# Second layer of the last two token tiles by seven block products each

## The chip, the cores and the metric

The kernel runs on one core of a Trainium2 chip. TensorE (PE) multiplies matrices, VectorE (DVE), ScalarE (ACT) and GpSimd (POOL) work elementwise, SyncE (SP) issues most transfers. Each engine takes its instructions in the order of the program and waits for the others by semaphores. The metric is the device time of one execution in microseconds; the kernel before takes 279.55 us (median of 3 runs, 279.43 to 279.59).

## The reference

Linear attention over 8 batches of 8 heads, 576 tokens and 64 columns a head, then two matrix layers with a leaky ReLU between them:

```python
q_s = softmax(q, axis=-1); k_s = softmax(k, axis=2)
kv = np.einsum('bhsd,bhse->bhde', k_s, v)
x = np.einsum('bhsd,bhde->bhse', q_s, kv)   # as 4608 tokens x 512
h = x @ w_in                                # 512 -> 2048
g = np.maximum(0.01 * h, h)
return g @ w_out                            # 2048 -> 512, float32
```

## The kernel before

The 4608 tokens are nine tiles of 512 (0 to 8). Attention fills `xT` (bf16, 128 partitions x 4 blocks of columns x 4608 tokens) some tiles ahead of the two layers. The first layer of a tile is 16 blocks of 128 of the 2048 hidden columns, four matmuls each, and a leaky activation by ACT into `g` tiles; the second layer is four groups of 128 tokens (`tsub`), 16 matmuls of 512 columns each, summed in one PSUM bank. All of it is bf16. The program is scheduled by hand: each engine's order is the order of the code.

The last two tiles, 7 (`TA`) and 8 (`TB`), go another way. The first layer of both together is a product of 2 x 2 blocks (tokens of tile 7 and 8; halves of the 512 input columns; hidden columns j and 8 + j), and Winograd's form needs seven block products for it, not eight, at the price of sums of blocks. Weight sums t1 to t4 come from GpSimd (`in_weight_sums`, L789; `last_weights`, L827, casts the block b22), token sums s1 to s4 from DVE (`token_sums`), stored as f32 (`F32R`); five of the seven products have such sums as operands, two are plain bf16. `pair_layer1(i)`, for i from 0 to 7, is one *block row*: seven products of two matmuls of 512 columns (`product`, L967), seven adds on DVE (L989), and four leaky activations. `pair_first(i + 1)` makes the first product of the next row and copies it by ACT to `e1` (L976). The last leaky of a row is held back into the next one (`held_leaky`). The hidden results go to `g7` (tile 7) and `g8` (tile 8), most of them into parts of `xT` that are no longer needed (`spent`).

Between the products PE gets *filling* matmuls, taken one by one from a generator (`fill_steps`): 48 of tile 6's second layer (`tsub` 1 to 3), then 16 of tile 7's (`pair_step`, L1027), eight a block row. Behind the last row come tile 7's other 48 matmuls (L1027) and its stores. Meanwhile DVE and ACT make the sums r1 to r4 and c22 of tile 8's hidden block for its second layer (L1070 to L1075). That layer is again a 2 x 2 product (halves of 256 tokens; halves of 2048 hidden columns; halves of 512 output columns) by seven products `product2` (L1091) of 16 matmuls of 256 columns: two in bf16 and five in f32, with weight sums v1 to v4 and o22 made earlier (`out_weight_sums`). DVE adds them up (L1101) and the results are stored (`put`, L1112).

PSUM: `psB_pool` has six banks, taken in turn, for every product; `psO_pool` has two, for the second layer's groups. A product waits until the bank of the sixth one before has been read. The raw input buffers (`raw_pool`, six) are taken over by the weight sums through `strip`; the pools of the attention part (`front`) are closed before `token_sums`, and the pools of the pair stage (`pairs`) before the last stage.

Of the kernel before, what the change touches and what calls it, by code (L numbers as in the profile page):

```python
# [20 lines left out]
L = 64  # L21
R = 9
# [4 lines left out]
def kernel(  # L27
# [37 lines left out]
    mx_pool = front.enter_context(tc.tile_pool(name="mx", bufs=1))  # L65
    small_pool = front.enter_context(tc.tile_pool(name="small", bufs=3))
    qT_pool = front.enter_context(tc.tile_pool(name="qT", bufs=2))

    psB_pool = ctx.enter_context(tc.tile_pool(name="psB", bufs=6, space=bass.MemoryType.PSUM))
    psO_pool = ctx.enter_context(tc.tile_pool(name="psO", bufs=2, space=bass.MemoryType.PSUM))  # L70
# [43 lines left out]


    XH, X8, XE = (slice(0, 7), slice(9, 16)), slice(7, 9), slice(16, 20)
    qe1 = const_pool.tile([P, XE.stop, P], BF16, name="qe1")
    vb2 = [const_pool.tile([P, R, 2, 2, D + 2], BF16, name=f"vb{i}") for i in range(2)]
# [689 lines left out]

    def in_weight_sums(i):
        w = lambda cs, fh: w_in_sb[:, cs, (fh * NH + i) * P : (fh * NH + i + 1) * P]  # L810
        if i == 0:
            late["t"] = strip("t")
# [17 lines left out]

    def token_sums():
        front.close()
        late["one"] = pool = pairs.enter_context(tc.tile_pool(name="late", bufs=1, reuse_waits="tile"))
        late["pool"] = pairs.enter_context(tc.tile_pool(name="late2", bufs=2, reuse_waits="tile"))
        for n in ("s1", "s2", "s3", "s4", "a22"):
# [124 lines left out]

    g7 = {}
    g8 = spent

    def product(w, a):
        ps = psB_pool.tile([P, TT], FP32, name="pp", tag=BANK_TAG)
# [12 lines left out]
    def pair_layer1(i, between):  # L978
# [3 lines left out]
        if i < 2:  # L982
            pair = g_pool.tile([P, 2, TT], BF16, name="gj")
            g7[i], g7[NH + i] = pair[:, 0], pair[:, 1]
        else:
            g7[i], g7[NH + i] = (spent(NF + 2 * (i - 2) + n) for n in range(2))

        def add(o, ps, e):
            nc.vector.tensor_tensor(out=o, in0=ps, in1=e, op=ALU.add)  # L989

        def do(w, a):
            ps = product(w, a)
            next(between)
            return ps

        add(u2, do(of(("t2", i)), of("s2")), e1)
        for fn in held_leaky:
            fn()
        add(e1, do(lambda c: w_in_sb[:, 2 + c, i * P : (i + 1) * P], lambda c: xT[:, 2 + c, XA]), e1)
        leaky(g7[i], e1)  # L1000
        add(u3, do(of(("t3", i)), of("s3")), u2)
        p5 = do(of(("t1", i)), of("s1"))
        add(u4, p5, u2)
        if i + 1 < NH:
            pair_first(i + 1)
            next(between)
# [4 lines left out]
        add(u3, do(of(("t4", i)), of("a22")), u3)  # L1011
        leaky(g8(i), u3)
        add(u4, do(of(("b22", i)), of("s4")), u4)
        held_leaky[:] = [lambda: leaky(g7[NH + i], u4)]
        if i + 2 < NH:
            in_weight_sums(i + 2)

    pouts, started = {}, [0] * NTS
    turn = [j for i in range(NH) for j in (i, NH + i)]

    def pair_step(tsub):
        j = turn[started[tsub]]
        started[tsub] += 1
        if tsub not in pouts:
            pool, tag = (psO_pool, "pout") if tsub < 2 else (psB_pool, BANK_TAG)
            pouts[tsub] = pool.tile([P, O], FP32, name="pout", tag=tag)
        nc.tensor.matmul(  # L1027
            pouts[tsub],
            lhsT=g7[j][:, tsub * P : (tsub + 1) * P],
            rhs=w_out_sb[:, j],  # L1030
            start=(started[tsub] == 1),
            stop=(started[tsub] == NF),
        )

    def fill_steps():
        for tsub in range(1, NTS):
            yield from layer2_at(TA - 1, g_sb, tsub)
        for tsubs in ((2, 3), (0, 1)):
            for _ in range(4):
                for tsub in tsubs:  # L1040
                    pair_step(tsub)
                    yield

    def between_products():
        fill = fill_steps()
        for n in range(NH):
            for k in range(7):
                for _ in range(1 + k // 6):
                    next(fill)
                yield  # L1050

    between = between_products()
    pair_first(0)
    next(between)
    for i in range(NH):
        pair_layer1(i, between)
    held_leaky[0]()
    next(between, None)
    pairs.close()
    pool = ctx.enter_context(tc.tile_pool(name="late3", bufs=1, reuse_waits="tile"))  # L1060
    quarter = lambda h, b, fh: xT[:, :, (2 * fh + b) * TT + h * M2 : (2 * fh + b) * TT + (h + 1) * M2]
    for n in ("r1", "r2", "r3", "r4", "c22"):
        late[n] = pool.tile([P, NH, M2], F32R, name=n)
    for first in (True, False):
        for b in range(2):
            o = lambda n: late[n][:, 4 * b : 4 * b + 4]
            part = lambda n: o(n).bitcast(FP32)
            a11, a12, a21, a22 = (quarter(h, b, fh) for h in range(2) for fh in range(2))
            if first:
                nc.scalar.copy(out=o("c22"), in_=a22)  # L1070
                nc.vector.tensor_tensor(out=o("r1"), in0=a21, in1=a22, op=ALU.add)
                nc.vector.tensor_tensor(out=o("r2"), in0=part("r1"), in1=a11, op=ALU.subtract)
            else:
                nc.vector.tensor_tensor(out=o("r3"), in0=a11, in1=a21, op=ALU.subtract)
                nc.vector.tensor_tensor(out=o("r4"), in0=a12, in1=part("r2"), op=ALU.subtract)  # L1075

    while started[0] < NF:
        for tsub in range(NTS):
            pair_step(tsub)
    for tsub in range(NTS):  # L1080
        store(TA * TT + tsub * P, pouts[tsub], nc.scalar.copy)

    def product2(a, w, each=False):
        if each:
# [15 lines left out]
    def add(o, ps, e):  # L1100
        nc.vector.tensor_tensor(out=o, in0=ps, in1=e, op=ALU.add)  # L1101

    rows = lambda n: (lambda m: late[n][:, m])
    plain_g = lambda fh: (lambda m: g8(fh * NH + m)[:, 0:M2])
    plain_w = lambda fh: (lambda m: w_out_sb[:, fh * NH + m, E1])
    out1, out2 = ([osb_pool.tile([P, O], FP32, name="out_sb") for _ in range(2)] for _ in range(2))
    e1, u2, u3, u4 = (g_pool.tile([P, 2, H2], FP32, name="gu", tag="gj") for _ in range(4))

    def put(o, half, i, cols):
        for n, issue in enumerate((nc.sync, nc.scalar)):  # L1110
            b, c = divmod(TB * TT + half * M2 + i * P + n * L, S)
            issue.dma_start(out=out_r[b, c // L, :, cols], in_=o[n * L : (n + 1) * L, cols])  # L1112

    nc.scalar.copy(out=e1, in_=product2(plain_g(0), plain_w(0)))
    ps = product2(plain_g(1), plain_w(1))
    for i in range(2):
        add(out1[i][:, E1], ps[:, i], e1[:, i])
        put(out1[i], 0, i, E1)
    add(u2, product2(rows("r2"), rows("v2")), e1)
    add(u3, product2(rows("r3"), rows("v3")), u2)  # L1120
    ps = product2(rows("r1"), rows("v1"))
    for i in range(2):
        add(out2[i][:, E2], ps[:, i], u3[:, i])
    add(u4, ps, u2)
    ps = product2(rows("c22"), rows("v4"))
    for i in range(2):
        add(out2[i][:, E1], ps[:, i], u3[:, i])
        put(out2[i], 1, i, slice(0, O))
    ps = product2(rows("r4"), rows("o22"), True)
    for i in range(2):  # L1130
        add(out1[i][:, E2], ps[i], u4[:, i])
        put(out1[i], 0, i, E2)
    assert not hooks, list(hooks)


# [28 lines left out]
```

## Time and profile before

| | before |
|---|---|
| median of 3 runs | 279.55 us |
| profiled execution | 279.63 us, of which the span from the first to the last instruction is 277.8 us |
| granted TensorE clock | 0.998 |
| TensorE weight loads (PEld) | 141.4 us, 51% of the span |
| HBM | 46 MB, 166 GB/s over the span |
| 210 to 249.8 us | block rows of tiles 7 and 8 with fillers |
| 249.8 to 260.2 us | tile 7's other 48 matmuls |
| 260.2 to 273.7 us | tile 8's seven products |
| 273.7 to 277.8 us | the last add and the last stores |

The profile is of one execution. Busy time is counted for each engine; a busy PE is not PE at its peak, as its matmuls are pipelined and their ends are modelled. In the timeline a matmul's time includes its way through the array, so successive starts tell its cost. The chain of waits follows the work that ended last back to its releaser. In rows of stretches the columns are PE, PEld, DVE, ACT and POOL (busy us and instructions), the clock, the DMA share and GB/s.

### The profile page before, as it was taken

How to read it: one execution, taken by the hardware profiler on the slowest of the kernel's cores; microseconds unless marked ns; L12 is line 12 of the kernel's file. 1: busy time of each engine (PE TensorE's matmuls, PEld its weight loads, DVE VectorE, ACT ScalarE, POOL GpSimd, SP SyncE). 2: the span in 40 equal slices, each digit the busy share in tenths (PEclk: the TensorE clock that was granted, in tenths of full speed). 3: DMA queues.
4: the chain of work that ended last, by engine and by line, in shares of the span. 5: the costliest groups of instructions: out<-in, count | busy, mean ns of one | idle time of the engine just before them, and what ended most of it. 6: DMA issues, size and time to landing. Idle time of an engine off the chain costs nothing.

```text
span 277.8 us, 5089 instructions
## 1 busy us (share of the span) xinstructions
PE 270.2 (97%) x1945; PEld 141.4 (51%) x1970; DVE 223.0 (80%) x310; ACT 166.2 (60%) x291; POOL 76.4 (28%) x97
## 2 busy tenths in 40 slices
PE   8899999999999999999999999999999999999994
PEld 3478644444444554445444444444445555554693
DVE  2986996999999959966885498967959999999542
ACT  4977573783488286755587448665674667655300
POOL 2957360159003002100500096003000856400000
PEclk9999999999999999999999999999999999999999
DMA  7999999987994499089409930330601011100243
GB/s 246 335 204 318 249 253 271 402 295 214 299 406 158 59 336 351 7 233 396 122 0 253 403 92 2 85 77 1 162 0 40 0 38 38 36 6 0 68 123 113
DMA packets 40167, 46.46 MB, mean 167 GB/s; under 512 B 18768, under 2 KB 23632, under 8 KB 40144
## 3 DMA queue, kind: packets, MB, share of 16 engines
q1 hardware_dynamic: 36160, 41.43, 47.5%
q0 software_dynamic: 3504, 4.20, 8.8%
q10 hardware_dynamic: 480, 0.52, 0.6%
q8 instruction: 15, 0.25, 0.3%
q14 instruction: 8, 0.07, 0.1%
HBM read 36.70 MB, written 9.44 MB: 166 GB/s over the span
## 4 chain that ended last, share of the span: by engine, by line
PE 93%; DVE 3%; DMA 2%; issue 1%; ACT 0%; SPq 0%; ACTq 0%
PE pout L583 35%; PE ph L562 35%; PE pp L967 9%; PE pout L1027 5%; PE pq L1091 5%; DMA k_raw<-in_k_dram 2%; PE po L478 2%; DVE t L159 1%; PE pokv L340 1%; PE pkv L340 1%; PE pkv L418 0%; DVE k_raw L409 0%; ACT ke L205 0%; DVE kmax L159 0%; ACT e L976 0%
## 5 line engine op out<-in xcount | busy, mean ns | idle before, releaser
L583 PE MATMUL pout<-w_out_sb,gj 128*128 128x512 bf16 x432 | 104.9, 380 | 1.0 <-issue 0.3
L562 PE MATMUL ph<-xT,w_in_sb 128*128 128x512 bf16 (+1 forms) x505 | 98.5, 352 | 0.4
L571 ACT ACTIVATE gj<-ph 128x512 bf16<-128x512 f32 x112 | 63.5, 602 | 19.1 <-PE ph L562 18.2
L562 PEld LDWEIGHTS <-w_in_sb 128*128 128x128 bf16 x512 | 49.7, 98 | 47.2 <-DMA w_in_sb<-in_moe_w_in_dram 0.3
L583 PEld LDWEIGHTS <-gj 128*128 128x128 bf16 x448 | 42.5, 98 | 54.8 <-issue 8.1
L217 POOL CAST vb<-v_raw 128x1152 bf16<-128x1152 f32 x13 | 21.8, 1707 | 81.9 <-DMA v_raw<-in_v_dram 81.9
L577 ACT COPY out_sb<-pout 128x512 f32<-128x512 f32 x28 | 16.0, 585 | 39.0 <-PE pout L583 20.4
L320 DVE TENSOR_REDUCE qsum<-qe 128x36 f32<-128x2304 bf16 (+5 forms) x13 | 20.0, 1542 | 6.2 <-ACT qe L311 6.1
L205 ACT ACTIVATE ke<-k_raw 128x2304 bf16<-128x2304 f32 (+2 forms) x13 | 18.0, 1383 | 9.4 <-DVE k_raw L197 9.0
L989 DVE TENSOR_TENSOR u<-pp,u 128x512 f32<-128x512 f32 x32 | 20.9, 685 | 1.4 <-PE pp L967 0.2
L327 DVE TENSOR_TENSOR qe<-qe,qrec 128x2304 bf16<-128x2304 bf16 (+5 forms) x13 | 21.5, 1657 | 0.4
L244 DVE TENSOR_REDUCE qmax<-q_raw 128x36 f32<-128x2304 f32 (+5 forms) x13 | 20.0, 1540 | 0.3 <-DMA q_raw<-in_q_dram 0.3
L311 ACT ACTIVATE qe<-q_raw 128x2304 bf16<-128x2304 f32 (+5 forms) x13 | 17.2, 1322 | 4.3 <-POOL q_raw L303 3.3
L967 PE MATMUL pp<-s,t 128*128 128x512 f32 x48 | 18.5, 486 | 0.0
L197 DVE TENSOR_TENSOR k_raw<-k_raw,kall 128x1152 f32<-128x1152 f32 (+2 forms) x10 | 18.1, 1821 | 0.3
L303 POOL TENSOR_TENSOR q_raw<-q_raw,qmax 128x512 f32<-128x512 f32 (+3 forms) x7 | 11.8, 1681 | 20.8 <-DVE qmax L244 20.3
L159 DVE TENSOR_TENSOR t<-t 128x256 f32<-128x256 f32 (+2 forms) x22 | 13.5, 615 | 0.7
L499 ACT CAST xT<-po 128x448 bf16<-128x448 f32 (+3 forms) x31 | 13.3, 515 | 1.3 <-PE po L478 1.3
L360 DVE RECIPROCAL krec<-pokv 128x2 f32<-128x2 f32 x8 | 1.3, 166 | 15.3 <-PE pokv L478 15.3
L303 DVE TENSOR_TENSOR q_raw<-q_raw,qmax 128x2304 f32<-128x2304 f32 (+1 forms) x6 | 13.2, 2202 | 0.2
L789 POOL TENSOR_TENSOR t<-w_in_sb 128x256 fp32r<-128x256 bf16 x16 | 11.4, 712 | 7.1 <-PE pp L967 7.1
L159 DVE TENSOR_TENSOR t<-k_raw 128x512 f32<-128x512 f32 (+1 forms) x11 | 12.1, 1102 | 1.2 <-DMA k_raw<-in_k_dram 1.0
(118 smaller groups left out, 306.0 us busy)
## 6 DMA issues: line engine op xcount, KB each, us to landing
out_dram<-out_sb SPq DMA_DIRECT2D x66, 128.0 KB, 2.7
q_raw<-in_q_dram SPq DMA_DIRECT2D x6, 1152.0 KB, 9.0
v_raw<-in_v_dram SPq DMA_DIRECT2D x6, 1152.0 KB, 11.3
k_raw<-in_k_dram SPq DMA_DIRECT2D x5, 1152.0 KB, 6.5
k_raw<-in_k_dram SPq DMA_DIRECT2D x6, 576.0 KB, 6.0
v_raw<-in_v_dram SPq DMA_DIRECT2D x4, 576.0 KB, 7.6
w_in_sb<-in_moe_w_in_dram POOLq DMA_DIRECT2D x7, 256.0 KB, 7.6
w_out_sb<-in_moe_w_out_dram POOLq DMA_DIRECT2D x6, 256.0 KB, 9.4
```

The costliest lines, as they stand in the source:

```text
L159: nc.vector.tensor_tensor(out=o, in0=i0, in1=i1, op=ALU.max)
L197: eng.tensor_tensor(out=ks, in0=ks, in1=st[b]["kall"][:, hs].unsqueeze(2).to_broadcast([P, n, R, D]), op=ALU.subtract,)
L217: eng.tensor_copy(out=o, in_=i)
L244: nc.vector.tensor_reduce(out=o, in_=st[b]["q"][:, hs, rs], axis=AX.X, op=ALU.max)
L303: eng.tensor_tensor(out=qs, in0=qs, in1=st[b]["qmax", rs.start, hs.start].unsqueeze(3).to_broadcast([P, m, n, D]), op=ALU.subtract,)
L320: nc.vector.reduce_sum(out=qsum, in_=q_cols(b, rs, hs), axis=AX.X)
L327: nc.vector.tensor_tensor(out=qes if out is None else out, in0=qes, in1=st[b]["qrec", rs.start, hs.start].unsqueeze(3).to_broadcast([P, n, ...
L562: nc.tensor.matmul(ph, lhsT=w_in_sb[:, cb, j * P : (j + 1) * P], rhs=xT[:, cb, c0 : c0 + n], start=(cb == 0 and first), stop=(cb == NB - 1 ...
L571: nc.scalar.activation(out=o, in_=ph, func=AF.Prelu, alpha=LEAKY_SLOPE)
L583: nc.tensor.matmul(pout, lhsT=g_sb[j // 2][:, j % 2, tsub * P : (tsub + 1) * P], rhs=w_out_sb[:, j, os], start=(j == 0), stop=(j == NF - 1),)
L967: nc.tensor.matmul(ps, lhsT=w(c), rhs=a(c), start=(c == 0), stop=(c == 1))
L989: nc.vector.tensor_tensor(out=o, in0=ps, in1=e, op=ALU.add)
```

## The change

Tile 7's second layer is also done by seven block products, at the end, beside tile 8's:

- Only the 48 matmuls of tile 6 are left as fillers: three ahead of the rows, one at each of three places in row 0, two at each of three places in rows 1 to 7. `pair_step` and its 64 matmuls of 512 columns are gone.
- In a block row the products come in the order p6, p7, fillers, p2, the next row's first, fillers, p5, p4, p3, fillers; the adds in the order u2, u3, e1, u4, c22, u3, u4.
- Tile 7's sums r1 and r3 are made by GpSimd in four pieces (`sums_ahead`): three behind the weight sums of rows 2, 4 and 6, the last behind the last row. Its r2 and r4 are made by DVE, c22 by ACT, in three pieces each, behind the rows.
- Behind the rows come fourteen products: first and second of tile 7 and 8 in turn, then the other five of tile 7 (p5, p6, p7, p4, p3), then the other five of tile 8. Tile 8's sums r1 to r4 are made by DVE between these, in the order r1, r2, r3, r4, and c22 by ACT.
- Tile 7's results are stored by SP, tile 8's by SP and ACT in turn.
- Buffers: `qe1` and `vb2` move into the pools that are closed early, a pool `late0` holds r1 and r3 of tile 7, and the raw buffer of the weight sums `t` is taken first, so that tile 8's r1 can take it over.

```diff
     def out_weight_tiles():
+        late["t"] = strip("t")
...
+    def sums_ahead(n):
+        if n == 0:
+            for name in ("r3", "r1"):
+                late_rows(name, name, late["ahead"])
+        (ms, h0), (_, h1) = g7_blocks(0)[n], g7_blocks(1)[n]
+        for name, x, y, op in (("r3", h0(0), h1(0), ALU.subtract), ("r1", h1(0), h1(1), ALU.add)):
+            nc.gpsimd.tensor_tensor(out=late[name][:, ms], in0=x, in1=y, op=op)
...
-        add(u2, do(of(("t2", i)), of("s2")), e1)
+        p6 = product(of(("t2", i)), of("s2"))
+        p7 = product(of(("t3", i)), of("s3"))
+        between(1 if i == 0 else 2)
+        add(u2, p6, e1)
         for fn in held_leaky:
             fn()
-        add(e1, do(lambda c: w_in_sb[:, 2 + c, i * P : (i + 1) * P], lambda c: xT[:, 2 + c, XA]), e1)
+        add(u3, p7, u2)
+        p2 = product(lambda c: w_in_sb[:, 2 + c, i * P : (i + 1) * P], lambda c: xT[:, 2 + c, XA])
+        add(e1, p2, e1)
         leaky(g7[i], e1)
-        add(u3, do(of(("t3", i)), of("s3")), u2)
-        p5 = do(of(("t1", i)), of("s1"))
-        add(u4, p5, u2)
         if i + 1 < NH:
             pair_first(i + 1)
-            next(between)
+        between(1 if i == 0 else 2)
+        p5 = product(of(("t1", i)), of("s1"))
+        p4 = product(of(("t4", i)), of("a22"))
+        p3 = product(of(("b22", i)), of("s4"))
+        between(1 if i == 0 else 2)
+        add(u4, p5, u2)
         add(c22, p5, u3)
...
+        if i in (2, 4, 6):
+            sums_ahead(i // 2 - 1)
...
+    sums_ahead(3)
     pairs.close()
...
-    while started[0] < NF:
-        for tsub in range(NTS):
-            pair_step(tsub)
...
+    def row_sums(wide, name, n, pool, op, x, y):
+        late_rows(name, n, pool)
+        for (ms, h0), (_, h1) in zip(wide(0), wide(1)):
+            view = lambda s: late[s][:, ms].bitcast(FP32) if isinstance(s, str) else (h0, h1)[s[0]](s[1])
+            o = late[name][:, ms]
+            if op is None:
+                nc.scalar.copy(out=o, in_=view(x))
+            else:
+                nc.vector.tensor_tensor(out=o, in0=view(x), in1=view(y), op=op)
...
+    def second(z):
+        for i in range(2):
+            add(z["o1"][i][:, E1], z["p2"][:, i], z["e1"][:, i])
+            put(z, z["o1"][i], 0, i, E1)
+
+    def sixth(z):
+        z["u2"], z["u4"], z["u3"] = gu(), gu(), gu()
+        add(z["u2"], z["p6"], z["e1"])
+        add(z["u4"], z["p5"], z["u2"])
+
+    def seventh(z):
+        add(z["u3"], z["p7"], z["u2"])
+        for i in range(2):
+            add(z["o2"][i][:, E2], z["p5"][:, i], z["u3"][:, i])
...
+    A["p1"] = product2(plain_g(ga, 0), plain_w(0))
+    first_two(A)
+    row_sums(g7_wide, "r2", "r2", last_pool, ALU.subtract, "r1", (0, 0))
+    B8["p1"] = product2(plain_g(gb, 0), plain_w(0))
+    first_two(B8)
+    row_sums(g7_wide, "c22", "c22", last_pool, None, (1, 1), None)
+    A["p2"] = product2(plain_g(ga, 1), plain_w(1))
+    second(A)
+    row_sums(g7_wide, "r4", "r4", last_pool, ALU.subtract, (0, 1), "r2")
+    B8["p2"] = product2(plain_g(gb, 1), plain_w(1))
+    second(B8)
+    A["p5"] = product2(rows("r1"), rows("v1"))
+    late["r1"] = strip("r1").rearrange("p a b -> p (a b)")[:, 0 : NH * M2].rearrange("p (m t) -> p m t", t=M2)
+    for (ms, h0), (_, h1) in zip(g8_wide(0), g8_wide(1)):
+        nc.vector.tensor_tensor(out=late["r1"][:, ms], in0=h1(0), in1=h1(1), op=ALU.add)
+    A["p6"] = product2(rows("r2"), rows("v2"))
...
+    sixth(A)
+    A["p7"] = product2(rows("r3"), rows("v3"))
+    row_sums(g8_wide, "r2", "r2", last_pool, ALU.subtract, "r1", (0, 0))
+    seventh(A)
+    A["p4"] = product2(rows("c22"), rows("v4"), True)
+    row_sums(g8_wide, "c22", "c22", last_pool, None, (1, 1), None)
+    A["p3"] = product2(rows("r4"), rows("o22"), True)
+    row_sums(g8_wide, "r3", "r3", ahead_pool, ALU.subtract, (0, 0), (1, 0))
+    fourth(A)
+    third(A)
+    B8["p5"] = product2(rows("r1"), rows("v1"))
+    B8["p6"] = product2(rows("r2"), rows("v2"))
+    row_sums(g8_wide, "r4", "r4", last_pool, ALU.subtract, (0, 1), "r2")
+    sixth(B8)
...
```

More of the change, by code (lines that the diff above doesn't have):

```diff
@@ L116 @@
     XH, X8, XE = (slice(0, 7), slice(9, 16)), slice(7, 9), slice(16, 20)
-    qe1 = const_pool.tile([P, XE.stop, P], BF16, name="qe1")
-    vb2 = [const_pool.tile([P, R, 2, 2, D + 2], BF16, name=f"vb{i}") for i in range(2)]
+    qe1 = fix_pool.tile([P, XE.stop, P], BF16, name="qe1")
+    vb2 = [fix_pool.tile([P, R, 2, 2, D + 2], BF16, name=f"vb{i}") for i in range(2)]
     kd0 = const_pool.tile([P, 2, 2, 2, D], BF16)
@@ L832, in token_sums @@
         front.close()
+        late["ahead"] = ctx.enter_context(tc.tile_pool(name="late0", bufs=1, reuse_waits="tile"))
         late["one"] = pool = pairs.enter_context(tc.tile_pool(name="late", bufs=1, reuse_waits="tile"))
@@ L1016, in pair_layer1 @@
             in_weight_sums(i + 2)
[L1018 to L1033, printed above, removed]
+        if i in (2, 4, 6):
+            sums_ahead(i // 2 - 1)
     def fill_steps():
@@ L1037, in fill_steps, with between @@
             yield from layer2_at(TA - 1, g_sb, tsub)
-        for tsubs in ((2, 3), (0, 1)):
-            for _ in range(4):
-                for tsub in tsubs:
-                    pair_step(tsub)
[L1042 to L1052, printed above, removed]
+    fill = fill_steps()
+    def between(n):
+        for _ in range(n):
+            next(fill)
     pair_first(0)
-    next(between)
+    between(3)
     for i in range(NH):
-        pair_layer1(i, between)
+        pair_layer1(i)
     held_leaky[0]()
-    next(between, None)
+    next(fill, None)
+    sums_ahead(3)
     pairs.close()
[L1060 to L1075, printed above, removed]
-    while started[0] < NF:
-        for tsub in range(NTS):
-            pair_step(tsub)
-    for tsub in range(NTS):
-        store(TA * TT + tsub * P, pouts[tsub], nc.scalar.copy)
+    last_pool = ctx.enter_context(tc.tile_pool(name="late3", bufs=1, reuse_waits="tile"))
     def product2(a, w, each=False):
@@ L1103 @@
     rows = lambda n: (lambda m: late[n][:, m])
-    plain_g = lambda fh: (lambda m: g8(fh * NH + m)[:, 0:M2])
+    plain_g = lambda g, fh: (lambda m: g(fh * NH + m)[:, 0:M2])
     plain_w = lambda fh: (lambda m: w_out_sb[:, fh * NH + m, E1])
[L1106 to L1111, printed above, removed]
-            issue.dma_start(out=out_r[b, c // L, :, cols], in_=o[n * L : (n + 1) * L, cols])
@@ L1114 @@
[L1114 to L1132, printed above, removed]
+    last_adds = lambda n: [last_pool.tile([P, O], FP32, name=f"{n}{i}") for i in range(2)]
+    gu = lambda: g_pool.tile([P, 2, H2], FP32, name="gu", tag="gj")
+    A = dict(t=TA, o1=[osb_pool.tile([P, O], FP32, name="out_sb") for _ in range(2)], issue=(nc.sync, nc.sync))
+    B8 = dict(t=TB, o1=last_adds("o1"), issue=(nc.sync, nc.scalar))
+    def put(z, o, half, i, cols):
+        for n, issue in enumerate(z["issue"]):
+            b, c = divmod(z["t"] * TT + half * M2 + i * P + n * L, S)
+            issue.dma_start(out=out_r[b, c // L, :, cols], in_=o[n * L : (n + 1) * L, cols])
@@ new lines, in fourth, with third @@
+    def fourth(z):
+        for i in range(2):
+            add(z["o2"][i][:, E1], z["p4"][i], z["u3"][:, i])
+            put(z, z["o2"][i], 1, i, slice(0, O))
+    def third(z):
+        for i in range(2):
+            add(z["o1"][i][:, E2], z["p3"][i], z["u4"][:, i])
+            put(z, z["o1"][i], 0, i, E2)
+    ga, gb = (lambda n: g7[n]), g8
+    ahead_pool = late["ahead"]
+    A["p1"] = product2(plain_g(ga, 0), plain_w(0))
+    first_two(A)
+    row_sums(g7_wide, "r2", "r2", last_pool, ALU.subtract, "r1", (0, 0))
@@ new lines @@
+    for (ms, h0), (_, h1) in zip(g8_wide(0), g8_wide(1)):
+        nc.vector.tensor_tensor(out=late["r1"][:, ms], in0=h1(0), in1=h1(1), op=ALU.add)
+    A["p6"] = product2(rows("r2"), rows("v2"))
+    A["o2"] = [osb_pool.tile([P, O], FP32, name="out_sb") for _ in range(2)]
+    B8["o2"] = last_adds("o2")
+    sixth(A)
[3 more added lines that the diff above has]
+    A["p4"] = product2(rows("c22"), rows("v4"), True)
@@ new lines @@
+    row_sums(g8_wide, "c22", "c22", last_pool, None, (1, 1), None)
[7 more added lines that the diff above has]
+    sixth(B8)
+    B8["p7"] = product2(rows("r3"), rows("v3"))
+    seventh(B8)
+    B8["p4"] = product2(rows("c22"), rows("v4"), True)
@@ L1133 @@
+    fourth(B8)
+    B8["p3"] = product2(rows("r4"), rows("o22"), True)
+    third(B8)
     assert not hooks, list(hooks)
```

50 lines of the change are left out of this document (36 added, 14 removed).

## The prediction

> **What bounds the kernel now.** I read the page's busy table and chain first, then the chain piece by piece from 210 us on, then the timeline of VectorE (DVE) and GpSimd (POOL) there.
>
> ```profile
> PE 270.2 (97%) x1945; PEld 141.4 (51%) x1970; DVE 223.0 (80%) x310; ACT 166.2 (60%) x291; POOL 76.4 (28%) x97
> PE 93%; DVE 3%; DMA 2%; issue 1%; ACT 0%; SPq 0%; ACTq 0%
> 220.00:230.00 10.00, 9.93 (x46) 5.37 (x45) 9.48 (x17) 6.63 (x12) 6.66 (x12) 1.00 0.11 26
> 250.00:260.00 10.00, 9.95 (x48) 4.52 (x47) 9.93 (x10) 3.66 (x6) 0.00 (x0) 1.00 0.01 2
> 260.00:270.00 10.00, 10.00 (x86) 9.42 (x85) 2.84 (x6) 2.61 (x5) 0.00 (x0) 1.00 0.53 131
> ```
>
> TensorE (PE) sets the end. But the average hides that DVE is nearly full from 220 to 260 (9.48 and 9.93 of 10) and loose only in the last stage (2.84). The change takes PE work out of the first of these stretches and puts DVE work into the last.
>
> ```profile
> 234.76 0.45 PE pout L583 x2
> 235.21 0.47 PE pp L967 x2
> 235.67 0.23 PE pout L583
> 236.60 0.43 PE pp L967 x2
> 239.75 0.45 PE pout L583 x2
> 249.78 3.25 PE pout L1027 x15
> 260.58 13.09 PE pq L1091 x112
> 273.70 0.42 DVE out_sb L1101
> ```
>
> These are pieces of the chain. From one pair of fillers (234.76) to the next (239.75) a block row takes PE 4.99: five f32 products of 0.465, two bf16 ones of 0.43, eight fillers of about 0.225. The 48 matmuls of tile 7 that follow run from 249.78 to about 260.2, 0.217 each; the last add starts at 273.70.
>
> ```profile
> 217.35 0.68 DVE L989 TENSOR_TENSOR u<-pp,e 128x512 f32<-128x512 f32 x1
> 218.13 0.69 DVE L989 TENSOR_TENSOR e<-pp,e 128x512 f32<-128x512 f32 x1
> 218.74 1.28 DVE L989 TENSOR_TENSOR u<-pp,u 128x512 f32<-128x512 f32 x2
> 219.94 0.68 DVE L989 TENSOR_TENSOR c<-pp,u 128x512 f32<-128x512 f32 x1
> 220.72 1.29 DVE L989 TENSOR_TENSOR u<-pp,u 128x512 f32<-128x512 f32 x2
> 221.93 0.68 DVE L989 TENSOR_TENSOR u<-pp,e 128x512 f32<-128x512 f32 x1
> 212.76 0.69 DVE L989 TENSOR_TENSOR u<-pp,e 128x512 f32<-128x512 f32 x1
> 249.84 1.29 DVE L989 TENSOR_TENSOR u<-pp,u 128x512 f32<-128x512 f32 x2
> ```
>
> One block row on DVE, with nothing idle: 4.58 from 217.35 to 221.93. Starts lie 0.60 apart, or 0.78 where an add touches what the add just ahead read or wrote. So DVE's floor for a row, 4.58, is 0.41 under PE's 4.99.
>
> **Block rows.** Two fillers a row go: PE 4.99 - 2 x 0.23 = 4.53. DVE keeps seven adds; in the new order (u2, u3, e1, u4, c22, u3, u4) two still follow their neighbour (u3 on u2, u3 on c22), so 4.58 stays. DVE becomes the pace. Its first add at 212.76 sits behind the s sums, which are untouched, so eight rows end at 212.76 + 8 x 4.58 = 249.40; the last add starts 0.60 earlier, 248.80, and ends at 249.48, where it ends at 251.13 now. That is 1.65 gained, not the 3.6 that PE is spared.
>
> **PE behind the rows.** Tile 7's 48 matmuls (10.4) leave; one more set of seven products comes.
>
> ```profile
> 260.42 3.66 PE L1091 MATMUL pq<-w_out_sb,xT 128*128 128x256 bf16 x32
> 263.83 5.99 PE L1091 MATMUL pq<-v,r 128*128 128x256 f32 x48
> 269.66 2.08 PE L1091 MATMUL pq<-v,c 128*128 128x256 f32 x16
> 271.58 2.08 PE L1091 MATMUL pq<-o,r 128*128 128x256 f32 x16
> ```
>
> By their starts, 32 bf16 matmuls take 3.41, so 1.71 a product; 16 f32 ones 1.92 (269.66 to 271.58). A set costs 2 x 1.71 + 5 x 1.92 = 13.02. PE's whole balance is -8 x 0.46 - 10.4 + 13.0 = -1.1: all that the change can give.
>
> When can PE begin? Tile 7's first product (A1) needs g7[7], the leaky of row 7's third add: 212.76 + 7 x 4.58 + 1.38 = 246.20, ends 246.89.
>
> ```profile
> 249.78 0.63 ACT L571 ACTIVATE xT<-c 128x512 bf16<-128x512 f32 x1 [1.16 <-DVE c L989]
> 229.77 0.06 issue
> 229.83 0.38 PE pout L583
> ```
>
> With 0.03 of handing over and 0.63 of leaky: 247.55. It feeds the eighth of A1's sixteen matmuls; nine of them and 0.06 end A1 at 248.57. Tile 8's first (B1) needs a leaky of the sixth add, 249.53: 250.55. Then A2 252.26, B2 253.97, tile 7's other five 263.57, tile 8's five 273.17. With 0.04 the last add starts at 273.21. If nothing else held PE, that is 0.49 earlier than now.
>
> **DVE and GpSimd behind the rows.** Here the wait is. Tile 7's r1 and r3 are summed by GpSimd in four pieces. Three run between rows; the last needs g7[15], the leaky of the very last add: 249.48 + 0.66 = 250.14. Then r3's piece, then r1's, and DVE's r2 needs r1.
>
> ```profile
> L272 POOL TENSOR_TENSOR qe<-qe,qrec 128x512 bf16<-128x512 bf16 x1 | 1.0, 1049 | 0.0
> L303 POOL TENSOR_TENSOR q_raw<-q_raw,qmax 128x512 f32<-128x512 f32 x3 | 3.1, 1040 | 14.6 <-DVE qmax L244 14.1 <-DVE krec L429 0.5
> 10.09 1.16 POOL L217 CAST vb<-v_raw 128x1152 bf16<-128x1152 f32 x1
> 160.18 5.26 POOL L217 CAST vb<-v_raw 128x1152 bf16<-128x1152 f32 x2 [23.64 <-DMA v_raw<-in_v_dram]
> 162.28 2.17 DVE L159 TENSOR_TENSOR t<-k_raw 128x1024 f32<-128x1024 f32 x1
> 251.05 1.22 DVE L1071 TENSOR_TENSOR r<-xT 128x1024 fp32r<-128x1024 bf16 x1
> ...
> 255.84 1.22 DVE L1074 TENSOR_TENSOR r<-xT 128x1024 fp32r<-128x1024 bf16 x1
> 256.97 1.22 DVE L1075 TENSOR_TENSOR r<-xT,r 128x1024 fp32r<-128x1024 bf16 x1
> ```
>
> A 128x512 sum took GpSimd 1.04 alone. Beside a DVE sum of two SBUF operands a cast took 2.63 (half of 5.26) where 1.16 was seen earlier, and that DVE sum 2.17 where 1.22 is seen at 251.05: both slow down. DVE will run r2's first two pieces at that moment. From 250.18, two pieces end at 252.26 undisturbed. If DVE's 1024-wide piece (from 250.00) stretches to 2.17, it ends at 252.17; GpSimd does 1.99 x 1.16/2.63 = 0.88 of its 2.08 by then and ends at 253.37. I take 1.25 a piece: T = 252.68, nearer the undisturbed row, since DVE overlaps only part.
>
> The Trainium skill, GPSIMD Engine Reference, Key points, speaks against this placement: GpSimd shares its SBUF interfaces with VectorE and contends with DVE instructions that have two SBUF inputs; the rows at 160.18 and 162.28 agree. By that rule the sum lies at the disturbed end below, 281.9, and without it at 280.8. Its Engine selection puts two-input work on GpSimd at about twice VectorE's time; as an estimate from that page, two pieces of 2 x 0.60 end at 252.58, and the sum would come out 0.1 lower.
>
> From T on DVE's queue is the path: 1.13 for a 1024-wide sum (255.84 to 256.97), 0.60 for 512, and for 256 wide 0.34, the 0.76 of two less one of 0.42:
>
> ```profile
> 269.86 0.76 DVE L1101 TENSOR_TENSOR out_sb<-pq,gu 128x256 f32<-128x256 f32 x2 [1.23 <-PE pq L1091]
> ```
>
> After r2's last piece (0.60): second(A) 0.68, r4 2.33 (pieces of 512, 1024, 512), second(B8) 0.68, tile 8's r1 2.26, u2 and u4 1.38, tile 8's r2 2.26, u3 0.78, the two output adds 0.76: 11.13. They read the bank of p5, which is the bank that the second half of tile 7's last product (p3) must take, six PSUM allocations on. So PE waits there: 252.68 + 0.04 + 0.60 + 11.13 = 264.45; 0.22 for restarting (0.06 + 0.38 - 0.22, the rows at 229.77), 0.96 for that half, 9.60 for tile 8's five, 0.04: last add at 275.27. PE alone was at 263.57 where this has 265.63: it loses 2.06. Behind it DVE has 8.8 us of work (two sums of 2.26, 1.36 of output adds, 1.38, 1.54) for 9.6 of PE, so nothing more is added.
>
> **Costed at nothing.** GpSimd's row with a sum takes 3.00 of weights (rows below) plus 2.1, the next one 3.00: 8.1 in 9.16; uncovered, the 2.1 would hold p6 two rows on. But p5, which frees the first buffer, ends 3.1 into a row, and of the 6.0 us left until that p6 the two sums that it needs take 1.4.
>
> ```profile
> 216.24 0.67 POOL L789 TENSOR_TENSOR t<-w_in_sb 128x256 fp32r<-128x256 bf16 x1
> 219.24 0.68 POOL L789 TENSOR_TENSOR t<-w_in_sb 128x256 fp32r<-128x256 bf16 x1
> ```
>
> ACT's copies of c22, about 2.1 a tile, lie behind the e1 copies and end near 253, products before p4; tile 8's need p4 of tile 7 gone and are wanted 6 us later. Tile 7's twelve stores all go to SP, which has nothing else left; the six that ACT issues for tile 8 wait for second(B8), and only those c22 copies stand behind them. The last two stores are the same as now. The moved buffers change owners long free by then.
>
> **Sum.** 275.27 - 273.70 = +1.57 on the profiled execution's 279.63 (span 277.8 and 1.83 around it): 281.2. The median shown, 279.55, is 0.08 lower, well inside the margin. Bounds: undisturbed GpSimd +1.15 (280.8), disturbed +2.26 (281.9); if r1 didn't matter at all, second(A) could begin at A2's end, 252.30, and the same queue gives +0.55 (280.2).
>
> **Rivals.** *r2 waits for the whole of r1.* I let r2's first two pieces run from 249.40 because waits seem kept by regions: in the rows ACT writes spent parts of xT while PE reads others without a stall. If the wait is by buffer instead, all 2.33 lie behind T, 1.73 more: 282.9. Against it speaks just that; for it, that r1 is one tile that another engine writes piece by piece while DVE reads it for the next sum, and no tile of this kind is in the trace.
>
> *PE stays the bound.* The mechanism: DVE's queue after T gets through 2.1 us sooner than its 11.13, or the bank comes free sooner, so the second half of p3 never waits. Then 273.21, or 279.63 - 0.49 = 279.1; it decides once those adds end before 262.4. For it: DVE is idle for most of 260 to 270 now, so it has time to catch up if any of these sums can start sooner than the queue's order lets it. Against: the pitches above are measured back to back, and the queue is full from T to the end of those adds.
>
> **How the numbers follow.** Forecast 0.55, whole buffer 0.22, PE bound 0.15, anything else 0.08. About 0.2%, 0.56, is what a measurement here tells from no change: 278.99 to 280.11. PE bound straddles its lower edge: 0.06 faster, 0.08 same; of the rest 0.03 faster and 0.04 same. That makes 0.09, 0.12, 0.79. The range, 279.4 to 283.2, takes the forecast's own 280.2 to 281.9, whole-buffer waits, and leaves out the fast half of the third case and contention on top of the second.
>
> **What would show it.** Right: rows 4.58 apart on DVE with no idle; a DVE idle stretch of about 1.5 before one 512-wide sum near 252, released by GpSimd; PE's only long wait, about 2, ahead of the last 8 f32 matmuls of tile 7, released by a DVE output add. Wrong: rows below 4.5, DVE idle in front of products from 255 to 264, or r2's first piece starting after GpSimd's last.

## The result, and the profile after

The changed kernel takes 280.89 us (median of 4 runs, 280.81 to 281.00), the kernel before 279.57 beside it: a ratio of 1.0048, with a 95% interval of 1.0036 to 1.0061. The profiled execution took 280.83 us with a span of 279.0. The forecast was 281.2 in a range of 279.4 to 283.2. The direction came out, and so did DVE's part of the path; the place where the time is lost did not, and that the sum still came within 0.4 us is in part luck.

The busy table and the chain of the changed kernel:

```profile
span 279.0 us, 5241 instructions
PE 270.0 (97%) x2018; PEld 148.7 (53%) x2018; DVE 229.2 (82%) x327; ACT 166.1 (60%) x291; POOL 84.2 (30%) x105
PE 88%; DVE 6%; DMA 2%; issue 1%; ACT 0%; SPq 0%; DVEq 0%
```

PE's busy time hardly moved; DVE has 6.2 us more and GpSimd 7.8. The chain now goes through DVE for 6% of the span, 3% before. DVE's timeline shows the block rows (start, duration, what):

```profile
212.89 0.68 DVE L1027 TENSOR_TENSOR u<-pp,e 128x512 f32<-128x512 f32 x1
...
217.47 0.68 DVE L1027 TENSOR_TENSOR u<-pp,e 128x512 f32<-128x512 f32 x1
218.26 0.69 DVE L1027 TENSOR_TENSOR u<-pp,u 128x512 f32<-128x512 f32 x1
...
222.05 0.68 DVE L1027 TENSOR_TENSOR u<-pp,e 128x512 f32<-128x512 f32 x1
...
236.93 0.69 DVE L1027 TENSOR_TENSOR u<-pp,u 128x512 f32<-128x512 f32 x1 [0.46 <-PE pp L1009]
...
248.69 1.29 DVE L1027 TENSOR_TENSOR u<-pp,u 128x512 f32<-128x512 f32 x2
```

A row is 4.58 on DVE (217.47 to 222.05) with no idle between. PE is spared about 0.46 of fillers in each of eight rows, but DVE sets the pace: the last add of the rows starts at 249.29 (the second of the pair at 248.69), where it started at 250.44, so only 1.15 is gained. One wait of 0.46 stands in row 5. Next, both engines behind the rows:

```profile
248.13 1.16 POOL L1004 TENSOR_TENSOR r<-xT 128x512 fp32r<-128x512 bf16 x1 [5.25 <-ACT xT L572]
250.72 2.01 POOL L1004 TENSOR_TENSOR r<-xT 128x512 fp32r<-128x512 bf16 x1 [1.44 <-ACT xT L572]
249.89 0.68 DVE L1108 TENSOR_TENSOR r<-r,gj 128x512 fp32r<-128x512 f32 x1
250.49 1.22 DVE L1108 TENSOR_TENSOR r<-r,xT 128x1024 fp32r<-128x1024 f32 x1
252.75 0.69 DVE L1108 TENSOR_TENSOR r<-r,xT 128x512 fp32r<-128x512 f32 x1 [1.05 <-POOL r L1004]
253.37 0.75 DVE L1098 TENSOR_TENSOR out_sb<-pq,gu 128x256 f32<-128x256 f32 x2
...
263.61 0.76 DVE L1098 TENSOR_TENSOR out_sb<-pq,gu 128x256 f32<-128x256 f32 x2
264.29 2.35 DVE L1108 TENSOR_TENSOR r<-xT 128x1024 fp32r<-128x1024 bf16 x2
...
270.15 2.01 DVE L1098 TENSOR_TENSOR gu<-pq,gu 128x512 f32<-128x512 f32 x3
272.19 2.21 DVE L1098 TENSOR_TENSOR o<-pq,gu 128x256 f32<-128x256 f32 x6
```

The last piece of r2 waits for GpSimd until 252.75, and from there DVE has no gap until 274.4. But PE does not wait for it. Its timeline and the end of the chain:

```profile
262.26 2.08 PE L1088 MATMUL pq<-o,r 128*128 128x256 f32 x16
264.18 5.92 PE L1088 MATMUL pq<-v,r 128*128 128x256 f32 x48
269.94 2.08 PE L1088 MATMUL pq<-v,c 128*128 128x256 f32 x16
250.09 23.86 PE pq L1088 x201
273.98 0.42 DVE o L1098
```

The sixteen matmuls of tile 7's p3 run from 262.26 and tile 8's p5 starts 1.92 later: no wait ahead of the second half. The last add starts at 273.98, only 0.28 later than before. So most of the 1.2 that the span has gained lies behind it, with the last eight stores. First the kernel before, then the changed one (first and last start in the fourth column):

```profile
L1112 SPq DMA_DIRECT2D out_dram<-out_sb x4: 467/512/551, 272.2 to 274.1; - x4
L1112 ACTq DMA_DIRECT2D out_dram<-out_sb x4: 497/560/795, 272.2 to 274.4; - x4
```

```profile
L1121 SPq DMA_DIRECT2D out_dram<-o x4: 468/550/556, 273.3 to 275.2; - x4
L1121 ACTq DMA_DIRECT2D out_dram<-o x4: 498/556/793, 273.3 to 275.4; - x4
```

Four stores stand on each queue, about 0.55 each. The first four of the eight start with p4's output adds, and those are the third and fourth of the six adds at 272.19, so they start at 272.87 and later, behind DVE's queue, though PE had finished the first half of p4 near 271.0. So the eight stores begin 1.1 later and the span ends 5.7 behind their start, as it ended 5.6 behind it before.

### The profile page after: what moved, and what is told of

Its sections match the earlier page's. It is cut to its first block, busy times and chain, and to the rows that moved or that the text cites. A ratio compares the mean times of both kernels' runs of the same rounds, so it can differ in the third digit from the quotient of the medians.

```text
span 279.0 us, 5241 instructions
## 1 busy us (share of the span) xinstructions
PE 270.0 (97%) x2018; PEld 148.7 (53%) x2018; DVE 229.2 (82%) x327; ACT 166.1 (60%) x291; POOL 84.2 (30%) x105
## 4 chain that ended last, share of the span: by engine, by line
PE 88%; DVE 6%; DMA 2%; issue 1%; ACT 0%; SPq 0%; DVEq 0%
PE ph L563 35%; PE pout L584 34%; PE pq L1088 9%; PE pp L1009 7%; DVE u L1027 3%; DMA k_raw<-in_k_dram 2%; PE po L479 2%; DVE t L160 1%; PE pokv L341 1%; PE pkv L341 1%; DVE c L1027 1%; PE pkv L419 0%; DVE k_raw L410 0%; ACT ke L206 0%; ACT xT L572 0%
## 5 line engine op out<-in xcount | busy, mean ns | idle before, releaser
L584 PE MATMUL pout<-w_out_sb,gj 128*128 128x512 bf16 x448 | 103.7, 380 | 0.0
L584 PEld LDWEIGHTS <-gj 128*128 128x128 bf16 x448 | 41.9, 98 | 51.9 <-issue 4.6
L218 POOL CAST vb<-v_raw 128x1152 bf16<-128x1152 f32 x13 | 19.6, 1536 | 83.7 <-DMA v_raw<-in_v_dram 43.6
L578 ACT COPY out_sb<-pout 128x512 f32<-128x512 f32 x24 | 14.0, 584 | 34.1 <-PE pout L584 20.3
L1009 PE MATMUL pp<-s,t 128*128 128x512 f32 x48 | 17.0, 458 | 0.0
L160 DVE TENSOR_TENSOR t<-t 128x256 f32<-128x256 f32 (+2 forms) x22 | 14.4, 654 | 0.7
L160 DVE TENSOR_TENSOR t<-k_raw 128x512 f32<-128x512 f32 (+1 forms) x11 | 11.2, 1016 | 1.1 <-DMA k_raw<-in_k_dram 1.0
L1088 PE MATMUL pq<-v,r 128*128 128x256 f32 x96 | 11.9, 284 | 0.0
```

The costliest lines, as they stand in the source:

```text
L160: nc.vector.tensor_tensor(out=o, in0=i0, in1=i1, op=ALU.max)
L218: eng.tensor_copy(out=o, in_=i)
L584: nc.tensor.matmul(pout, lhsT=g_sb[j // 2][:, j % 2, tsub * P : (tsub + 1) * P], rhs=w_out_sb[:, j, os], start=(j == 0), stop=(j == NF - 1),)
L1009: nc.tensor.matmul(ps, lhsT=w(c), rhs=a(c), start=(c == 0), stop=(c == 1))
L1088: nc.tensor.matmul(ps[i], lhsT=a(m)[:, i * P : (i + 1) * P], rhs=w(m), start=(m == 0 and (each or i == 0)), stop=(m == NH - 1 and (each or ...
```

## The experiments

Two theories were put to the test. A: DVE's queue behind the rows sets the end, by way of tile 8's stores. B: PE's products set the end. Ratios are to the kernel before, measured beside each, with 95% intervals; for each the diff against the changed kernel is shown. The kernel before had two executions near 281.5 among the 31 beside the first four experiments, and two among the 25 beside the next four. They pull those ratios down a little: by medians the row order is at 1.0001, the gap and row order at 0.9990 and no r3 at 1.0009.

| run | median us | ratio | first of the last eight stores | last add | span |
|---|---|---|---|---|---|
| before, profiled | | 1 | 272.2 | 273.70 | 277.8 |
| changed, profiled | 280.89 | 1.0048 (1.0036 to 1.0061) | 273.3 | 273.98 | 279.0 |
| r1 first | 281.59 | 1.0073 (1.0049 to 1.0097) | 274.07 | 274.6 | 279.8 |
| r3 by GpSimd | 280.89 | 1.0051 (1.0034 to 1.0067) | 273.18 | 275.17 | 279.1 |
| row order | 279.38 | 0.9994 (0.9978 to 1.0010) | 271.67 | 272.59 | 277.5 |
| held banks | 280.85 | 1.0044 (1.0028 to 1.0060) | 273.13 | 274.97 | 278.9 |
| gap filled | 280.76 | 1.0046 (1.0029 to 1.0063) | 272.97 | about 273.6 | 278.7 |
| gap and row order | 279.04 | 0.9978 (0.9956 to 1.0000) | 271.58 | 272.83 | 277.4 |
| no r3 | 279.55 | 1.0004 (0.9987 to 1.0020) | 271.88 | 273.88 | 277.8 |
| sums by DVE | 284.24 | 1.0165 (1.0126 to 1.0204) | | | 282.4 |
| u4 late | 280.66 | 1.0039 (1.0025 to 1.0053) | 272.58 | about 273.9 | 278.5 |
| r1's end by DVE | 280.68 | 1.0043 (1.0031 to 1.0056) | 273.07 | 274.00 | 278.8 |
| all together | 279.18 | 0.9991 (0.9978 to 1.0004) | 271.07 | 272.94 | 277.5 |
| changed again | 280.85 | 1.0049 (1.0036 to 1.0062) | 273.17 | | 279.0 |

In these traces DVE's first add of the rows starts anywhere from 212.49 to 212.91, so absolute times of two runs can differ by 0.4 for no reason in the edit. Counted from that add, the first of the last eight stores comes after 60.42 in the changed kernel (both traces), 60.44 with the gap filled, 60.16 with r1's end by DVE, 59.90 with u4 late, 59.18 with the row order, 59.10 without r3 and 61.36 with r1 first.

**Which bank a product takes.** The prediction let banks go round in turn. The built program assigns each product a PSUM bank; for the changed kernel:

```
tile 7:  p5 -> 4   p6 -> 0   p7 -> 3   p4 -> 5, 2   p3 -> 1, 0
tile 8:  p5 -> 3   p6 -> 4   p7 -> 5   p4 -> 2, 1   p3 -> 0, 4
```

The second half of p3 has bank 0, that of p6, whose last reader is the u2 add, and not bank 4 of p5, which DVE reads until 264.37. By this list banks are handed on in the order of their last readers. The list itself stands in no trace, but the traces bear it out where they can: the second half of p3 starts without a wait while DVE still reads the bank of p5, and in two runs below (r1 first, r3 by GpSimd) PE stands ahead of tile 8's p5 until the add has read tile 7's p7, the two that share bank 3. To see the wait that was forecast, DVE reads the banks of p6 and p7 once more:

```diff
     seventh(A)
+    held_banks = last_pool.tile([P, 2], FP32, name="hb")
+    for n, ps in enumerate((A["p6"], A["p7"])):
+        nc.vector.tensor_copy(out=held_banks[:, n : n + 1], in_=ps[:, 0, 0:1])
     A["p4"] = product2(rows("c22"), rows("v4"), True)
```

> Two one-column copies by DVE read the banks of tile 7's p6 and p7 once more behind the output adds, so that by the order of last readers the second half of p3 has to take p5's bank: the wait that the prediction put there, now made on purpose. If banks go by last reader, PE now stands before that half for about 1.3 us (the adds end near 264.4, it began at 263.2) and the last product ends that much later: 282.0 to 282.3. If a bank's turn were fixed (every sixth product), the wait would have been in the changed kernel already and nothing moves: 280.9 to 281.2, the copies alone.

```profile
263.31 0.75 DVE L1098 TENSOR_TENSOR out_sb<-pq,gu 128x256 f32<-128x256 f32 x2
264.12 1.22 PE L1088 MATMUL pq<-o,r 128*128 128x256 f32 x8 [1.04 <-DVE out_sb L1098]
```

In this kernel that half has bank 4, and the timeline shows PE idle for 1.04 ahead of it, released by those output adds; the last add starts 1.0 later, at 274.97. The mechanism is as forecast once the bank is the one assumed. But the time did not move: 280.85 is the time that was expected for a fixed turn, without a wait, and neither half of the expectation had a wait that costs nothing. The first of the last eight stores still came at 273.1, and the span ended 3.9 behind the last add and 5.8 behind that store. So PE has about 1 us of room in the changed kernel. That speaks for A.

**DVE's queue, moved by a GpSimd sum.**

```diff
-        for name, x, y, op in (("r3", h0(0), h1(0), ALU.subtract), ("r1", h1(0), h1(1), ALU.add)):
+        for name, x, y, op in (("r1", h1(0), h1(1), ALU.add), ("r3", h0(0), h1(0), ALU.subtract)):
```

> GpSimd sums r1's pieces ahead of r3's. Theory A (DVE's queue behind the rows sets the end, by way of tile 8's stores): the 1.05 us that DVE waits for GpSimd at 252.75 shrinks to about 0.1, but its next add waits for tile 7's second product (252.76 in the trace), so the queue comes 0.5 to 0.6 us earlier and so does the end: 280.3. Theory B (PE's products set the end, DVE is never late for them): the same time, 280.9.

It went the other way, 0.7 slower. The timeline says why:

```profile
250.53 3.12 POOL L1004 TENSOR_TENSOR r<-xT 128x512 fp32r<-128x512 bf16 x2 [6.86 <-ACT xT L572]
252.57 1.63 DVE L1108 TENSOR_TENSOR r<-r,xT 128x512 fp32r<-128x512 f32 x1 [1.04 <-POOL r L1004]
```

In the changed kernel r3's last piece had run early, at 248.13, since it needs only g7[0] to g7[7]. Now it stands behind r1's, beside DVE's last piece of r2, and that took 1.63 where it took 0.69, 0.94 more. Counted from the first add of the rows, the first of the last stores came 0.94 later too, and the median rose by 0.7. PE waited only 0.24. So most of a delay of DVE there is paid at the end: A, by an effect that the expectation had missed.

**Less for DVE, more for GpSimd.** Tile 8's r3 goes to GpSimd:

```diff
-    row_sums(g8_wide, "r3", "r3", ahead_pool, ALU.subtract, (0, 0), (1, 0))
+    late_rows("r3", "r3", ahead_pool)
+    for (ms, h0), (_, h1) in zip(g8_wide(0), g8_wide(1)):
+        nc.gpsimd.tensor_tensor(out=late["r3"][:, ms], in0=h0(0), in1=h1(0), op=ALU.subtract)
```

> Tile 8's r3 (two 1024-wide sums) is made by GpSimd, which is idle there, so DVE has 2.26 us less to do behind 264.3. Theory A: the first output add of tile 8's p4 follows that product (about 271.2) and not DVE's queue (272.87), the last eight stores start about 1.2 us earlier, and the end too: 279.7, less if GpSimd and DVE slow each other down around 261. Theory B: 280.9.

```profile
260.33 4.30 DVE L1108 TENSOR_TENSOR r<-r,xT 128x1024 fp32r<-128x1024 f32 x2
260.36 6.28 POOL L1181 TENSOR_TENSOR r<-xT 128x1024 fp32r<-128x1024 bf16 x2 [7.93 <-PE pq L1088]
265.29 6.01 PE L1088 MATMUL pq<-v,r 128*128 128x256 f32 x48 [1.24 <-DVE gu L1098]
```

The time is that of B, but not for B's reason: DVE's two sums of r2 beside it took 4.30 where they take 2.35, which gave 1.95 of the 2.26 back, and PE now waited 1.24 for a bank. By itself this run tells A and B apart no more. The next one does.

**The same sum left out.** Tile 8's r3 isn't computed and p7 takes tile 7's, so that no engine has more to do:

```diff
-    row_sums(g8_wide, "r3", "r3", ahead_pool, ALU.subtract, (0, 0), (1, 0))
```

> Tile 8's r3 sum is left out (its seventh product takes tile 7's r3), so DVE has 2.26 us less behind 264.3 and no other engine has more. Theory A: the output adds of tile 8 follow PE, the end is that of the last add at 273.98 with the 4.1 us behind it that the kernel before has: 279.9 to 280.1. Theory B: 280.8.

```profile
270.77 1.62 DVE L1098 TENSOR_TENSOR o<-pq,gu 128x256 f32<-128x256 f32 x4
271.88 2.91 SPq L1121 DMA_DIRECT2D out_dram<-o  x4
272.92 0.42 DVE L1098 TENSOR_TENSOR o<-pq,gu 128x256 f32<-128x256 f32 x1 [0.54 <-PE pq L1088]
273.88 0.42 DVE L1098 TENSOR_TENSOR o<-pq,gu 128x256 f32<-128x256 f32 x1 [0.53 <-PE pq L1088]
```

279.55, level with the kernel before and 0.35 under the least that A had expected. The last add is where it was; the stores start 1.4 earlier, and DVE's last adds wait for PE again (0.54 and 0.53). The span now ends 3.9 behind the last add. B would have kept 280.8. A is shown: the loss of the change lies in DVE's queue ahead of tile 8's first stores.

**The stores alone.** The same amount of work on DVE, but tile 8's u4 add behind p4's output adds:

```diff
         add(z["u2"], z["p6"], z["e1"])
-        add(z["u4"], z["p5"], z["u2"])
+        if z is A:
+            add(z["u4"], z["p5"], z["u2"])
...
     fourth(B8)
+    add(B8["u4"], B8["p5"], B8["u2"])
```

> Tile 8's last u4 add, which only the very last output adds need, stands behind the first stores' adds: the same work, so that the first of the last eight stores can start about 0.5 us earlier. Theory A (the end hangs on when DVE starts the stores of p4, as those are issued one behind the other ahead of the last ones): 0.4 to 0.6 us less than the changed kernel in the same call. If the end hung on the last add alone (about 273.98 in both): no change.

```profile
272.58 2.83 ACTq L1121 DMA_DIRECT2D out_dram<-o  x4
```

The first store came at 272.58, 0.6 before that of the changed kernel measured beside it, and the profiled span fell by 0.5, but the median by 0.2 only (280.66 for 280.85; single runs 280.21 to 280.80). The sign is A's, the size less than half of the 0.4 to 0.6 expected.

**The gap filled.** r4's first pieces stand in the wait for GpSimd. `part_sums` makes the named pieces of a sum of tile 7 on DVE, as `row_sums` makes all three:

```diff
-    row_sums(g7_wide, "r2", "r2", last_pool, ALU.subtract, "r1", (0, 0))
+    for n in ("r2", "r4"):
+        late_rows(n, n, last_pool)
+    part_sums("r2", "r1", (0, 0), (0, 1))
+    part_sums("r4", (0, 1), "r2", (0, 1))
+    part_sums("r2", "r1", (0, 0), (2,))
+    part_sums("r4", (0, 1), "r2", (2,))
```

> DVE makes the first two pieces of tile 7's r4 (which need only the first two of r2) while it waits for GpSimd, ahead of r2's last piece: the same work in another order, no engine changed. Theory A (DVE's queue behind the rows sets the end by way of tile 8's stores): the 1.05 us of waiting is used, tile 8's r1 starts 1.0 us earlier (256.0 for 257.03), the last eight stores start about 1.0 earlier, and the time is 279.7 to 279.9. Theory B (PE's products set the end): 280.8, as PE has no wait there.

```profile
250.36 2.01 POOL L1004 TENSOR_TENSOR r<-xT 128x512 fp32r<-128x512 bf16 x1 [1.43 <-ACT xT L572]
251.27 1.65 DVE L1160 TENSOR_TENSOR r<-gj,r 128x512 fp32r<-128x512 bf16 x1
```

Nothing was gained, and 280.76 is B's figure. But the first store came no earlier either (60.44 for 60.42, counted from the first add), so the edit did not shorten DVE's queue and cannot decide between the two: the piece put into the gap took 1.65 for 0.69, until 0.55 behind GpSimd's end, and eats the wait. With r1's last piece given to DVE instead, GpSimd has nothing to sum at that moment:

```diff
-            nc.gpsimd.tensor_tensor(out=late[name][:, ms], in0=x, in1=y, op=op)
+            if (n, name) != (3, "r1"):
+                nc.gpsimd.tensor_tensor(out=late[name][:, ms], in0=x, in1=y, op=op)
...
+    part_sums("r2", "r1", (0, 0), (0, 1))
+    part_sums("r1", (1, 0), (1, 1), (2,), ALU.add)
+    part_sums("r2", "r1", (0, 0), (2,))
```

> The last piece of tile 7's r1 is summed by DVE, between r2's second and third piece, and GpSimd sums nothing behind the rows while DVE has sums of two SBUF operands. If the two slow each other down, DVE's sums keep 1.13 and 0.60, r2's last piece starts about 0.35 us earlier, and the time is 0.3 to 0.4 less than the changed kernel's in the same call. If contention plays no part there, DVE's extra 0.60 and the 0.18 for following its neighbour eat most of the 1.05 of waiting all the same: 0.2 less at most.

```profile
250.52 1.22 DVE L1161 TENSOR_TENSOR r<-r,xT 128x1024 fp32r<-128x1024 f32 x1
251.65 0.69 DVE L1161 TENSOR_TENSOR r<-xT 128x512 fp32r<-128x512 bf16 x1
252.37 0.69 DVE L1161 TENSOR_TENSOR r<-r,xT 128x512 fp32r<-128x512 f32 x1
```

DVE's sums kept 1.22 and 0.69, and r2's last piece came 0.4 earlier against the start of the rows, as the first side expected. But the gain in time is 0.17, within the 0.2 that the second side allowed, so the time does not tell the two apart.

**GpSimd's share undone.** All of r1 and r3 by DVE, in the same places:

```diff
-            nc.gpsimd.tensor_tensor(out=late[name][:, ms], in0=x, in1=y, op=op)
+            nc.vector.tensor_tensor(out=late[name][:, ms], in0=x, in1=y, op=op)
```

> Tile 7's r1 and r3 are summed by DVE in the same places, none by GpSimd: eight sums of 512, 1.2 us behind rows 2, 4, 6 and behind the last. Theory A (DVE is the bound from the first row to the stores): 3.6 us more in the rows, and at the end 1.2 more for 1.05 of waiting saved: 284.3 to 284.6. If PE bounds the rows, DVE has 0 to 0.1 us of room in a row, so it would be nearly as much; if DVE were loose, 280.8.

284.24, 3.4 over the changed kernel and just under the 284.3 expected: sums put on DVE between the rows are paid at nearly their full length. Giving them to GpSimd is what keeps the change near the kernel before.

**The rows.** Two adds change places:

```diff
+        add(u4, p3, u4)
         add(u3, p4, u3)
         leaky(g8(i), u3)
-        add(u4, p3, u4)
```

> In a block row the last u4 add stands ahead of the last u3 add, so that u3 no longer follows the c22 add that reads it; no work is added or taken away. Theory A (DVE paces the rows at 4.58 us): a row falls to 4.40 on DVE, PE's 4.50 becomes the pace, rows end 1.0 to 1.4 us earlier, and everything behind them: 279.6 to 280.0. A rival, that PE paces the rows already and the 4.58 is its own: rows stay at 4.58 and the time at 280.9.

```profile
216.87 0.68 DVE L1027 TENSOR_TENSOR u<-pp,e 128x512 f32<-128x512 f32 x1
...
221.25 0.68 DVE L1027 TENSOR_TENSOR u<-pp,e 128x512 f32<-128x512 f32 x1
...
235.55 0.69 DVE L1027 TENSOR_TENSOR u<-pp,u 128x512 f32<-128x512 f32 x1 [0.47 <-PE pp L1009]
...
265.35 6.38 SPq L1121 DMA_DIRECT2D out_dram<-out_sb  x8
271.82 2.55 SPq L1121 DMA_DIRECT2D out_dram<-o  x4
```

A row is 4.38, and the time 279.38, 1.5 less than the changed kernel, a little better than expected, and level with the kernel before (0.9994). The rows were DVE's, not PE's: PE keeps up with 4.38, so its own pace is at most that, and not the 4.50 expected. SP is busy with tile 7's eight stores until 271.73, and tile 8's first on SP follows at 271.82, so from here on that queue stands close behind DVE's. With the gap filled as well (this edit and that of the gap, both as above):

> The row order (last u4 add ahead of the last u3) and r4's first pieces in the gap, together. Theory A: the gains add until PE is the limit: the first of the last eight stores comes at about 270.3 for 271.67, the last add at 272.6 as with the row order alone, the end about 0.9 earlier than that: 278.3 to 278.6, faster than the kernel before. Theory B: nothing over the row order alone, 279.4.

279.04, the lowest of all, where 278.3 to 278.6 had been expected. Its ratio of 0.9978 has an interval that reaches 1.0000, and by medians it is 0.1% under the kernel before: no difference that can be told. Together with r1's end by DVE and the late u4 (four edits, all shown above):

> Row order, r1's last piece by DVE with r4's first two pieces ahead of it, and tile 8's u4 late, together. Theory A: the stores of tile 8 start at PE's pace, about 270.2, and the end follows the last product: 278.3 to 278.7, 0.2 to 0.4% under the kernel before. If the row order is all that there is to gain: 279.3.

```profile
265.28 6.37 SPq L1122 DMA_DIRECT2D out_dram<-out_sb  x8
...
271.07 2.80 ACTq L1122 DMA_DIRECT2D out_dram<-o  x4
...
271.75 3.05 SPq L1122 DMA_DIRECT2D out_dram<-o  x4
```

279.18, 0.9991 of the kernel before: no difference that can be told, and near the 279.3 that the other side expected. Tile 8's first store left at 271.07 on ACT's queue, not at 270.2, and SP is still issuing tile 7's eight stores until 271.65, so SP's first of tile 8 leaves at 271.75; the next wait is there. No kernel was found that is clearly faster than the one before. As a measure of all this, the changed kernel was run again:

> The changed kernel itself, on the same chip as the three above, as their measure: 280.6 to 280.9, 1.0048 of the kernel before.

It gave 280.85, 1.0049.

## Why the prediction was right, and where it was not

- *Rows at DVE's pace:* right, 4.58 forecast and measured, and shown by the row order. The last add came 0.49 later than the 248.80 forecast (the second of the pair at 248.69, so 249.29): a start 0.13 later and the wait of 0.46 in row 5, less 0.10 as the eight rows without that wait took 36.54 and not 36.64.
- *PE's row of 4.53:* too high, since PE kept up with rows of 4.38 in the row order. It did no harm, as DVE was the bound.
- *GpSimd's end T:* 252.68 forecast, 252.73 measured, but by two errors that cancel. r3's last piece needs no g7[15] and ran early in 1.16; r1's was stretched to 2.01, more than the 1.25 taken.
- *r2's first pieces ahead of T:* right, they ran at 249.89 and 250.49. The rival of a wait for the whole buffer is out.
- *DVE's queue of 11.13:* 11.00 from 253.37 to 264.37.
- *PE alone, 273.21:* too early. PE did run without a wait from 250.09 on, and the last add came at 273.98. The hidden block that tile 8's first product waits for came 0.56 later than forecast (250.09 for 249.53), and the products behind it took 0.2 longer (23.86 for 23.64).
- *"They read the bank of p5, which is the bank that the second half of tile 7's last product (p3) must take":* this step failed. Banks go by last reader, that half takes p6's, and PE did not stand still there; the 2.06 of PE's loss that were the sum's main term are not there.
- *"The last two stores are the same as now", and 8.8 us of DVE work hidden under 9.6 of PE:* this failed too. As PE was not held up, DVE was behind it, by about 1.9 at tile 8's p4 (272.87 for about 271.0), and so the eight stores, which go out one by one, began 1.1 late. The comparison took the wrong mark: the first of these stores hang on the first half of p4, which PE reaches 6.7 behind the start of tile 8's five products, and not on the whole 9.6.

The result, +1.2 in the span for +1.57 forecast, is the sum of +0.28 at the last add and +0.9 behind it (5.0 for 4.1). The bound was named rightly, DVE from the rows to the end; of the two ways in which its lateness can reach the end, a bank or a store, the wrong one was taken. The last add was forecast 1.29 too late and the end behind it 0.9 too short, and that these nearly cancel is luck. In the runs of the table that have both, the end is the later of 5.6 to 5.9 behind the first of the eight stores and about 3.9 behind the last add, but for the last combination: there it is 5.7 behind the first of SP's four, 271.75. By this the forecast's own last add, 275.27, would have put the end at about 279.2, only 0.2 behind the measured one; the held banks, with a wait half as long, show the two ends level.

PE as the bound, 279.1, was the rival on the other side. The left-out sum, 279.55, shows that the kernel goes to PE's bound once DVE has 2.3 us less: there DVE's last adds wait for PE. The row order, 279.38, does not reach it: DVE is still without a gap until 272.3.

## What to carry to other kernels

When work is taken from a full engine, read the engine that is second in that stretch: here DVE's row was only 0.41 under PE's, and 3.7 us of saved fillers brought the rows to their end 1.15 earlier. Where that engine sets the pace, the order of its adds counts: to keep one add a row from following the one whose operand it writes took off about as much as the whole change had cost. At the end of a kernel, count the stores that still have to be issued, not the last instruction alone, and see what starts the first of them.

## What the runs showed of the hardware

*Two engines on SBUF.* A DVE sum of two SBUF operands that starts while a GpSimd sum runs is held until that is nearly done (0.69 became 1.63 and 1.65, both ending 0.55 behind GpSimd's), while one that is already running keeps its 1.22 and GpSimd's is stretched (1.16 to 2.01). DVE's adds with a PSUM operand in the rows kept 0.68 beside GpSimd. The Trainium skill, GPSIMD Engine Reference, Key points, names this contention, for DVE instructions with two SBUF inputs; the runs agree and give the price.

*Neighbours on DVE.* An add that needs what the add just ahead of it read or wrote starts 0.78 behind it, not 0.60; one such pair fewer in each of eight rows took 1.5 us off the kernel. The Trainium skill, VectorE: DVE Perf Modes, The DRAIN you can't avoid, states of eight copies that a semaphore after each of them costs nothing extra; that is another case than these adds, and no run here repeats it.

*Left open:* the wait of 0.46 or 0.47 on DVE in row 5. It stands at the same add with either row order and is put down to PE, but that add's own product had ended some 2 us earlier.
